# An extra 4 KB load of w1, issued by ACT between its two x loads, in a LayerNorm-MLP kernel

## The chip, the cores and the metric

The kernel runs on one core of a Trainium2 chip. A core has five engines with instruction queues of their own: TensorE (PE in the profile; its weight loads are listed apart as PEld), VectorE (DVE), ScalarE (ACT), GpSimd (POOL) and SyncE (SP). Transfers between DRAM and the on-chip memory (SBUF) are issued by an engine's queue and carried out by 16 DMA engines. Engines wait for one another through semaphores. The metric is the device time of one execution in microseconds, lower is better; the median of three runs is given.

## What is computed

x is 1 x 2048 x 1024, w1 is 1024 x 3584, w2 is 3584 x 1024, all in bf16.

```python
def reference(x, w1, b1, w2, b2):
    y = _layernorm(x, axis=-1)
    h = _gelu(jnp.einsum("bsd,df->bsf", y, w1) + b1)
    return jnp.einsum("bsf,fd->bsd", h, w2) + b2
```

The LayerNorm has no scale or shift of its own (eps 1e-5), and the GELU is the tanh form.

## The kernel before

The 2048 rows of x are 16 tiles of 128 rows; four tiles make a block of 512. The 1024 columns are eight row blocks of w1 ("t" or "dt", 128 rows each, 128 x 3584 x 2 = 917,504 bytes apart in DRAM), and the 3584 hidden columns are 28 groups "r" of 128. For each block of x the kernel makes the first product for all 28 groups (`pe_cell`, L330: w1 is the stationary operand, the transposed tile yT the moving one, eight matmuls to a group), applies bias and GELU on ACT (L350) into hT, and makes the second product (`out_chunk`, L379), to which DVE adds b2 (L390) before SP stores it. All of w1, w2 and x stay in SBUF once loaded.

The order on every engine is written by hand into five programs (`sp`, `pe`, `act`, `dve`, `pool`), lists of operations with the names of the events they wait for and signal. `_resolve` turns each name into a semaphore and a count, and `_emit` writes each list out in order: an engine stops at an operation until the events it names are there. `dma(dst, src, sig, nbytes, q)` (L177 and L178) appends one load to the SP list, or to the queue given as `q`, with a semaphore of its own. `est`, which `dma` fills from the sum of bytes, is a planned time by which the DVE's later operations are interleaved (L521 to L536); the first tiles' order does not depend on it.

**The loads at the start.** x tiles 0 and 1 come in halves of 512 columns: SP issues x0_0 and x1_0, ACT issues x0_1 and x1_1 (L200 to L203). Then, all on SP: w1 chunks 0, 1 and 2 (w1c0 to w1c2: two row blocks each, the first 512 columns; L204), x tile 2, w1c3, x tile 3, w1c4 and w1c5 (columns 512 to 768), b1, the other w1 chunks, x block 1, w2 in four chunks, b2, and x blocks 2 and 3.

**The first tile's way.** After its loads ACT loads its activation table (L399) and sums the first half of x tile 0 (L400); DVE sums the other half (L402) and subtracts the mean (L407, y0, in two parts). For tile 1 DVE makes the sum (L412) and the centred tile (L416, y1), in `raw_tile`; tile 2 follows in the same way. Tiles 0 to 2 of the first block are multiplied without their scale, which DVE applies to the product later (L347).

**The PE's opening.** 37 fill matmuls on constants (L290), the transposes of tile 0 (T0, L304), and then the steps of `OPEN` (L22): an entry (t, a, b) stands for tile t's matmuls with row blocks a to b for four groups r, and (t, None) for the transposes of tile t (T1, T2). ACT copies each transposed group from PSUM into yT (L310).

```python
OPEN = ((0, 0, 2), (1, None), (0, 2, 4), (0, 4, 6), (1, 0, 6), (0, 6, 8), (2, None), (1, 6, 8), (2, 0, 8))
```

So the (0,0,2) cells need w1c0, the (0,2,4) cells w1c1, the (0,4,6) cells w1c2 and the (0,6,8) cells w1c3; T1 needs y1, and T2 needs y2.

Of the kernel before, what the change touches and what calls it, by code (L numbers as in the profile page):

```python
# [7 lines left out]
BF16 = mybir.dt.bfloat16  # L8
# [3 lines left out]
P = 128  # L12
# [12 lines left out]
GROUPS_1 = ((0, 4, 6), (4, 8, 7))  # L25
GROUPS_2 = ((0, 2, 4), (2, 5, 5), (5, 8, 6))
NOB = 2
TAIL_CUTS = (0, 384, 512)
N_W2_CHUNKS = 4

# [56 lines left out]
def bass_standalone__mixer_channel_mlp__prompt_kernel(  # L87
# [13 lines left out]
    DT = D // P  # L101
# [32 lines left out]
    w1v = w1.rearrange("(t p) f -> p t f", p=P)  # L134
    w2v = w2.rearrange("(t p) d -> p t d", p=P)

    with ExitStack() as es:
        sb = lambda name, shape, dt: es.enter_context(nc.sbuf_tensor(name, shape, dt))
# [5 lines left out]
        hT_sb = sb("hT_sb", [P, FT, TB], BF16)  # L144
        o_sb = sb("o_sb", [P, NOB, D], BF16)
        b2_sb = sb("b2_sb", [P, D], BF16)
        c_sb = sb("c_sb", [P, NRAW, D], BF16)
        b1r_sb = sb("b1r_sb", [32, P], BF16)
        b1h_sb = sb("b1h_sb", [P, 32], BF16)
        b1_sb = sb("b1_sb", [P, 32], F32)  # L150
        junk_a = sb("junk_a", [P, HC], BF16)
        junk_d = sb("junk_d", [P, HC], BF16)
        ident = sb("ident", [P, P], BF16)
# [14 lines left out]
        act = _Prog("s_act")  # L168
# [8 lines left out]
        def dma(dst, src, sig, nbytes, q=None):  # L177
            (q or sp).op(lambda e, dst=dst, src=src: e.dma_start(dst, src), sig=sig, sem="d_" + sig, inc=16)  # L178
            dma_bytes[0] += nbytes
            est[sig] = DMA_T0 + dma_bytes[0] / DMA_BYTES_PER_US  # L180
# [18 lines left out]

        for i in range(2):  # L200
            for h, q in enumerate((sp, act)):
                dma(x_sb[:, i, h * HC:(h + 1) * HC], xf[i * P:(i + 1) * P, h * HC:(h + 1) * HC],
                    f"x{i}_{h}", P * HC * 2, q)  # L203
        for ci in range(3):  # L204
# [164 lines left out]
        def out_chunk(b, st, c0, c1, region, prev_store):  # L369
            ti = b * TPB + st  # L370
            ob = ti % NOB
            g = grp_n[0]
            grp_n[0] += 1
            bank = NRING + g % 2
            sig = f"m2_{ti}_{c0}"
            waits = [f"w2c{ci}" for ci in range(nw2c)]
            waits.append(grp_oe[g - 2] if g >= 2 else bank_gelu[bank])
            for ft in range(FT):
                pe.op(lambda e, st=st, ft=ft, c0=c0, c1=c1, bank=bank: e.matmul(  # L379
                    ps[:, bank, 0:c1 - c0], lhsT=hT_sb[:, ft, st * P:(st + 1) * P], rhs=w2_sb[:, ft, c0:c1],  # L380
                    start=(ft == 0), stop=(ft == FT - 1)),
                    waits=(waits if ft == 0 else []) + [hT_row[(b, ft)]],
                    sig=(sig if ft == FT - 1 else None))
            pe_t[0] += FT * _mm_us(c1 - c0)
            est[sig] = pe_t[0]
            dwaits = [sig, "b2"]
            if prev_store is not None:
                dwaits.append(prev_store)
            oe = f"oe_{ti}_{c0}"
            crit.append((est[sig], (lambda e, ob=ob, c0=c0, c1=c1, bank=bank: e.tensor_tensor(  # L390
                out=o_sb[:, ob, c0:c1], in0=ps[:, bank, 0:c1 - c0], in1=b2_sb[:, c0:c1], op=ALU.add),
                dwaits, oe, 0.2 + (c1 - c0) * 1e-3), b))
            grp_oe.append(oe)
            sev = f"st_{ti}_{c0}"
            sp.op(lambda e, ti=ti, ob=ob, c0=c0, c1=c1: e.dma_start(of[ti * P:(ti + 1) * P, c0:c1], o_sb[:, ob, c0:c1]),
                  waits=[oe], sig=sev, sem=f"d_st_{ob}_{region}", inc=16)
            store_last[(ob, region)] = sev
# [96 lines left out]
        for b in range(NB):  # L494
# [11 lines left out]
            for st in range(TPB):  # L506
                for dh in range(DH):
                    c0, c1 = dh * NCH, (dh + 1) * NCH
                    ob = (b * TPB + st) % NOB
                    prev = store_last.get((ob, dh))  # L510
                    last = (b == NB - 1 and st == TPB - 1 and dh == DH - 1)
                    if last:
                        for k, (a0, a1) in enumerate(zip(TAIL_CUTS[:-1], TAIL_CUTS[1:])):
                            out_chunk(b, st, c0 + a0, c0 + a1, dh if k == 0 else f"{dh}p{k}", prev)
# [65 lines left out]
```

## Time and profile before

| | before |
|---|---|
| median of 3 runs | 398.07 us (397.82 to 398.11) |
| profiled execution: its own time | 398.39 us |
| profiled execution: span | 397.2 us |
| granted TensorE clock | 1.00 |
| PE busy | 392.3 us (99%) |
| DVE, ACT, POOL busy | 156.6, 82.7, 9.5 us |
| DMA packets, bytes | 17357, 23.62 MB |
| HBM read, written | 19.14 MB, 4.19 MB |

The span is the time from the first to the last instruction that the profiler recorded; the execution's own time also holds what lies around it, here 1.19 us. The load engines are busy nearly all of the first 50 us, as the page's slices show, of 9.9 us each:

```profile
DMA  8999940000000000000000000000000000000000
GB/s 257 353 386 386 387 164 15 26 26 16 26 1 2 0 0 2 27 15 26 26 15 0 0 2 0 11 17 26 15 26 13 2 0 0 2 13 26 15 26 26
```

The row for the loads by queue shows who issues: q1 is SP's queue, q10 is ACT's, and q8 and q14 are fetches of instructions:

```profile
q1 hardware_dynamic: 17050, 23.08, 16.7%
q8 instruction: 15, 0.25, 0.3%
q10 hardware_dynamic: 288, 0.26, 0.2%
q14 instruction: 4, 0.03, 0.0%
```

ACT's 288 packets are the 256 pieces of x0_1 and x1_1, of 1 KB each, and 32 packets that report their arrival (16 to a load).

### The profile page before, as it was taken

Reading aid. Unit: us, or ns where it says so; the run is one execution under the profiler, and the core shown is the slowest. Engines: PE = TensorE matmul, PEld = TensorE weight load, DVE = VectorE, ACT = ScalarE, POOL = GpSimd, SP = SyncE. Lnnn points to the kernel's source line nnn. Section 1 sums busy time; section 2 is a strip of 40 time slices with the busy share of each in tenths; the row PEclk is TensorE's granted clock in tenths of the full one; section 3 lists DMA queues with packets and bytes.
Section 4 is the critical chain, followed back from the end, with each engine's and each line's share of the span. In section 5 each row is a group of like instructions: output and inputs, shape, how many; then the busy total and the mean of one; then the engine's idle time right before and its main releaser. Section 6 shows DMA issues by size and latency. Waiting matters only on the chain.

```text
span 397.2 us, 4608 instructions
## 1 busy us (share of the span) xinstructions
PE 392.3 (99%) x1968; PEld 187.9 (47%) x2003; DVE 156.6 (39%) x341; ACT 82.7 (21%) x125; POOL 9.5 (2%) x25
## 2 busy tenths in 40 slices
PE   8999999999999999999999999999999999999998
PEld 8844444444444444444444444444444444444445
DVE  4957889988999405988100000001100000001011
ACT  4264430000134442000024433100003334400000
POOL 0201100011000100000000000000000000000000
DMA  8999940000000000000000000000000000000000
GB/s 257 353 386 386 387 164 15 26 26 16 26 1 2 0 0 2 27 15 26 26 15 0 0 2 0 11 17 26 15 26 13 2 0 0 2 13 26 15 26 26
DMA packets 17357, 23.62 MB, mean 59 GB/s; under 512 B 1082, under 2 KB 9786, under 8 KB 17338
## 3 DMA queue, kind: packets, MB, share of 16 engines
q1 hardware_dynamic: 17050, 23.08, 16.7%
q8 instruction: 15, 0.25, 0.3%
q10 hardware_dynamic: 288, 0.26, 0.2%
q14 instruction: 4, 0.03, 0.0%
HBM read 19.14 MB, written 4.19 MB: 59 GB/s over the span
## 4 chain that ended last, share of the span: by engine, by line
PE 97%; DMA 1%; issue 1%; SPq 0%; DVE 0%
PE ps L379 49%; PE ps L330 48%; DMA w_sb<-in_w_dram 1%; SPq L178 0%; PE ps L304 0%; DVE o_sb L390 0%
## 5 line engine op out<-in xcount | busy, mean ns | idle before, releaser
L330 PE MATMUL ps<-yT_sb,w_sb 128*128 128x512 bf16 (+2 forms) x989 | 193.9, 355 | 1.2
L379 PE MATMUL ps<-w_sb,hT_sb 128*128 128x512 bf16 (+2 forms) x908 | 193.3, 373 | 0.8
L330 PEld LDWEIGHTS ps<-yT_sb,w_sb 128*128 128x128 bf16 x1008 | 92.5, 98 | 101.4 <-DMA w_sb<-in_w_dram 0.6
L379 PEld LDWEIGHTS ps<-w_sb,hT_sb 128*128 128x128 bf16 x924 | 89.2, 98 | 104.5
L350 ACT ACTIVATE hT_sb<-ps,b_sb 128x512 bf16<-128x512 f32 x112 | 76.2, 688 | 255.9 <-PE ps L330 231.8
L390 DVE TENSOR_TENSOR o_sb<-ps,b_sb 128x512 bf16<-128x512 f32 (+2 forms) x33 | 22.3, 675 | 198.9 <-PE ps L379 198.8
L277 DVE STREAM_TRANSPOSE yT_sb<-x_sb 32x256 bf16<-32x256 bf16 x192 | 83.7, 436 | 21.6 <-PE ps L330 18.6
L231 DVE BATCH_NORM_STATS2 st_sb<-x_sb 128x6 f32<-128x512 bf16 x32 | 20.9, 668 | 0.1
L347 DVE TENSOR_TENSOR ps<-ps,rbc_sb 128x384 f32<-128x384 f32 x28 | 15.2, 563 | 9.4 <-PE ps L330 9.0
L235 POOL TENSOR_TENSOR rstd_sb<-mv_sb,nhalf 128x1 f32<-128x1 f32 x16 | 8.7, 549 | 124.2 <-DVE mv_sb L238 124.1
L245 DVE TENSOR_SCALAR x_sb<-x_sb,mv_sb,rstd_sb 128x1024 bf16<-128x1024 bf16 x13 | 7.1, 545 | 2.8 <-POOL rstd_sb L235 2.0
L310 ACT COPY yT_sb<-ps 128x384 bf16<-128x384 bf16 (+2 forms) x10 | 4.5, 504 | 6.8 <-PE ps L304 6.8
L290 PE MATMUL ps<-const-bfloat16-1.0 128*128 128x128 bf16 x39 | 4.5, 310 | 0.8 <-PEq L565 0.8
L290 PEld LDWEIGHTS ps<-const-bfloat16-1.0 128*128 128x128 bf16 x39 | 4.1, 145 | 0.8 <-issue 0.8
L238 DVE BATCH_NORM_AGGREGATE mv_sb<-st_sb 128x2 f32<-128x15 f32 x16 | 3.5, 217 | 0.8
L304 PE MATMUL ps<-ident,c_sb 128*128 128x128 bf16 x24 | 2.4, 249 | 0.1
L402 DVE TENSOR_SCALAR_CACHE_REDUCE junk_d<-x_sb 128x512 bf16<-128x512 bf16 x1 | 0.7, 686 | 3.7 <-DMA x_sb<-in_x_dram 3.7
L304 PEld LDWEIGHTS ps<-ident,c_sb 128*128 128x128 bf16 x24 | 1.8, 111 | 0.3 <-issue 0.3
L412 DVE SCALAR_TENSOR_TENSOR junk_d<-x_sb 128x512 bf16<-128x512 bf16 x2 | 1.4, 688 | 1.1 <-DMA x_sb<-in_x_dram 1.1
L399 ACT ACT_TABLE_LOAD x1 | 1.3, 1283 | 1.7 <-PEq L565 1.7
L446 DVE STREAM_TRANSPOSE rbc_sb<-rs_sb 32x96 f32<-32x96 f32 x4 | 1.1, 270 | 0.1
L416 DVE TENSOR_SCALAR c_sb<-x_sb,sum_sb 128x1024 bf16<-128x1024 bf16 x2 | 1.0, 487 | 0.1
(22 smaller groups left out, 6.8 us busy)
## 6 DMA issues: line engine op xcount, KB each, us to landing
w_sb<-in_w_dram SPq DMA_DIRECT2D x4, 1792.0 KB, 18.5
w_sb<-in_w_dram SPq DMA_DIRECT2D x2, 2048.0 KB, 14.4
out_dram<-o_sb SPq DMA_DIRECT2D x31, 128.0 KB, 1.7
x_sb<-in_x_dram SPq DMA_DIRECT2D x3, 1024.0 KB, 14.5
w_sb<-in_w_dram SPq DMA_DIRECT2D x6, 256.0 KB, 5.5
w_sb<-in_w_dram SPq DMA_DIRECT2D x1, 1024.0 KB, 9.3
x_sb<-in_x_dram SPq DMA_DIRECT2D x2, 256.0 KB, 5.7
w_sb<-in_w_dram SPq DMA_DIRECT2D x1, 512.0 KB, 6.4
```

The lines of the kernel that those rows point to most:

```text
L231: return (lambda e, i=i, h=h: e.bn_stats(st_sb[:, i, 6 * h:6 * (h + 1)], x_sb[:, i, h * HC:(h + 1) * HC]), [x_ev.get(i, f"x{i}_{h}")], f"s ...
L235: pool.op(lambda e, i=i: e.tensor_tensor(out=rstd_sb[:, i:i + 1], in0=mv_sb[:, i, 1:2], in1=nhalf[:, i:i + 1], op=ALU.pow), waits=[f"mv{i} ...
L245: return (lambda e, i=i: e.tensor_scalar(out=x_sb[:, i, :], in0=x_sb[:, i, :], scalar1=mv_sb[:, i, 0:1], scalar2=rstd_sb[:, i:i + 1], op0= ...
L277: res.append((lambda e, src=src, dst=dst: e.transpose(out=dst, in_=src), waits, (f"tr{i}" if lastop else None), 0.47))
L290: pe.op(lambda e: e.matmul(ps[:, 0, 0:P], lhsT=one, rhs=one, start=True, stop=True), waits=[gate] if gate else [])
L304: pe.op(lambda e, j=j, o=(j - j0) * P: e.transpose(out=bap[:, o:o + P], in_=src[:, j * P:(j + 1) * P], identity=ident[:, :]), waits=waits, ...
L310: act.op(lambda e, dst=dst, psrc=psrc: e.copy(out=dst, in_=psrc), waits=[f"tp{i}_{j0}"], sig=f"te{i}_{j0}")
L330: pe.op(lambda e, b=b, r=r, dt=dt, n0=n0, n1=n1, bank=bank: e.matmul(ps[:, bank, n0:n1], lhsT=w1_sb[:, dt, r * P:(r + 1) * P], rhs=yT_sb[: ...
L347: crit.append((est[sig], (lambda e, bank=bank: e.tensor_tensor(out=ps[:, bank, 0:n], in0=ps[:, bank, 0:n], in1=rb, op=ALU.mult), [sig, "rb ...
L350: act.op(lambda e, r=r, bank=bank: e.activation(out=hT_sb[:, r, :], in_=ps[:, bank, :], func=ACT.Gelu_apprx_tanh, bias=b1_sb[:, r:r + 1], ...
L379: pe.op(lambda e, st=st, ft=ft, c0=c0, c1=c1, bank=bank: e.matmul(ps[:, bank, 0:c1 - c0], lhsT=hT_sb[:, ft, st * P:(st + 1) * P], rhs=w2_s ...
L390: crit.append((est[sig], (lambda e, ob=ob, c0=c0, c1=c1, bank=bank: e.tensor_tensor(out=o_sb[:, ob, c0:c1], in0=ps[:, bank, 0:c1 - c0], in ...
```

## The change

One load is added to ACT's list, between x0_1 and x1_1. It reads 16 elements (32 bytes) from each of 16 rows (every eighth) of each of the eight row blocks of w1, 128 pieces and 4096 bytes in all, into a new tile `touch_sb` of 16 partitions. Nothing reads this tile, and nothing waits for its semaphore. ACT issues x1_1 and all that follows after it.

```diff
+TOUCH = 16
...
+        touch_sb = sb("touch_sb", [16, DT, TOUCH], BF16)
...
         for i in range(2):
             for h, q in enumerate((sp, act)):
+                if i == 1 and q is act:
+                    dma(touch_sb[:, :, :], w1v[0:P:P // 16, :, 0:TOUCH], "touch", 16 * DT * TOUCH * 2, q)
                 dma(x_sb[:, i, h * HC:(h + 1) * HC], xf[i * P:(i + 1) * P, h * HC:(h + 1) * HC],
                     f"x{i}_{h}", P * HC * 2, q)
```

`w1v` is w1 seen as `(t p) f -> p t f` with p = 128 (L134), so partition p of the touch holds row 8p of every row block.

## The prediction

> **What bounds the kernel now.** I read the chain of waits first, then the start of that chain in order of time, then the start of all engines, then the load engines in short stretches. The page's chain:
>
> ```profile
> PE 97%; DMA 1%; issue 1%; SPq 0%; DVE 0%
> PE ps L379 49%; PE ps L330 48%; DMA w_sb<-in_w_dram 1%; SPq L178 0%; PE ps L304 0%; DVE o_sb L390 0%
> ```
>
> 97% is matmul. The change touches none of it, so only the other 3% can move. In order of time (start, length, what):
>
> ```profile
> 1.64 0.05 issue
> 1.69 0.43 SPq L178
> 2.12 0.04 issue
> 2.16 0.47 SPq L178
> 2.63 0.04 issue
> 2.67 5.29 DMA w_sb<-in_w_dram
> 7.96 0.05 issue
> 8.00 2.41 PE ps L330 x40
> ```
>
> The third w1 piece (w1c2, issued by SP at 2.67) lands at 7.96 and releases the PE at 8.00; from there the chain is PE to the end, but for gaps of 0.05 and the last store. So the end moves one for one with the PE's start at 8.00, and nothing after it can be won by this change. The timeline up to there (start, length, instruction, idle time before):
>
> ```profile
> 0.78 0.89 ACTq L178 DMA_DIRECT2D x_sb<-in_x_dram  x2
> ...
> 1.70 1.28 ACT L399 ACT_TABLE_LOAD   x1 [1.70 <-PEq L565]
> ...
> 3.57 0.63 ACT L400 ACTIVATE junk_a<-x_sb 128x512 bf16<-128x512 bf16 x1 [0.58 <-DMA x_sb<-in_x_dram]
> ...
> 5.20 0.68 DVE L412 SCALAR_TENSOR_TENSOR junk_d<-x_sb 128x512 bf16<-128x512 bf16 x1
> ...
> 6.41 0.64 PE L330 MATMUL ps<-yT_sb,w_sb 128*128 128x128 bf16 x8
> 6.83 0.49 PEld L304 LDWEIGHTS ps<-ident,c_sb 128*128 128x128 bf16 x8
> ```
>
> Issues and landings by the DMA view: ACT issues x0_1 at 0.78 (0.41 us) and x1_1 at 1.22 (0.46); x1_1 lands 3.4 us later, at 4.62. w1c0, w1c1, w1c2 land at 6.39, 7.26 and 7.96 (issue at 1.69, 2.16, 2.67 plus 4.7, 5.1, 5.3). The load engines in stretches of half a microsecond (the last two columns are their busy share and GB/s):
>
> ```profile
> 1.75:2.25 0.50, 0.50 (x7) 0.50 (x6) 0.00 (x0) 0.50 (x1) 0.00 (x0) 1.00 0.82 45
> ...
> 2.75:3.25 0.50, 0.50 (x8) 0.50 (x6) 0.00 (x0) 0.23 (x1) 0.00 (x0) 1.00 1.09 377
> 3.25:3.75 0.50, 0.50 (x7) 0.50 (x6) 0.01 (x1) 0.18 (x1) 0.00 (x0) 1.00 1.04 295
> 3.75:4.25 0.50, 0.50 (x8) 0.50 (x6) 0.50 (x1) 0.50 (x2) 0.00 (x0) 1.00 0.92 248
> 4.25:4.75 0.50, 0.50 (x7) 0.41 (x4) 0.39 (x3) 0.04 (x1) 0.00 (x0) 1.00 0.95 285
> ```
>
> Two cold starts show here. In 1.75 to 2.25 the engines are 82% busy and move 45 GB/s: the DMA view of that stretch has 22 packets at 81.8% of 16 engines, so 0.818 x 16 x 0.5 / 22 = 0.30 us for each 1 KB piece, the first of x. And from 3.25, when w1's first pieces come up, the rate falls to 295, 248, 285, then 324 and 326, and is 358 on average from 5.75 to 8.25; the shortfall is (63+110+73+34+32) x 0.5 / 358 = 0.44 us. It isn't even: by the sums of these rates the bytes of x0, x1 and w1c0 (786 KB) have moved by about 4.85, but w1c0 lands at 6.39, 1.5 us later, while x1 landed 0.7 us after its bytes. The trace's arrival times agree: 14 of w1c0's 16 parts arrive by 5.37, two at 6.35 and 6.36. This lag of about a microsecond on two engines stays with w1c1 and w1c2, and so sets the 8.00.
>
> **The change part by part.** Removed: nothing. Added: one issue on ACT, 128 pieces of 32 bytes and 16 arrivals on the load engines; moved: x1_1's issue and what ACT does after it.
>
> ACT's issue: the nearest rows are the other L178 issues, 0.41 to 0.57 us while the queue is open, and 1.20 for b1 (28 pieces, at 5.87, with a backlog ahead). I take 0.45. Queued behind it on ACT: x1_1's issue (1.22 to 1.67), the table load (1.70 to 2.15, end 3.43) and L400, which waits for x0_0 until 3.57. The 0.58 idle hides it: cost 0. At 1.20 the table load would end at 4.18 and y0 come 0.55 late; the PE has 0.4 us between its T0 transposes (the last starts near 6.0) and 6.41, and 0.2 before 8.00, so even that ends near 0.
>
> x1_1: lands at 4.62 + 0.45 = 5.07 if the touch itself takes little. L412 for tile 1 begins at 5.20, when the DVE is free, so it is hidden. After that cover, L412 (0.69 + 0.08) and L416 (0.49) give y1 at 6.41, and T1 is loaded at 6.83: another 0.42. So x1_1 may land as late as about 5.6 before T1 is late, and T1 may be 0.2 late before w1c2's matmuls are.
>
> The touch on the load engines: 8 pieces and one arrival on each. Lower bound: 256-byte pieces in the last store, 144 packets at 18.7% of 16 engines over 0.8 us, 0.187 x 16 x 0.8 / 144 = 17 ns each; nine on each engine are 0.15 us. Upper bound: x's first pieces, 0.30 us; eight are 2.4 us. Engines are busy from 1.75 on (0.98 of 1.70 to 8.20), so this is paid by the SP queue's loads too, w1c2 among them. In the stretch 2.25 to 3.25 SP's queue has 55.8% and ACT's 37.9% of the same 16 engines.
>
> A rule that speaks against the change: the Trainium skill, "DMA: Bandwidth & Descriptors", section "Issuing engines are not separate DMA queues", says that loads issued from any engine run on the same 16 engines and interleave, so another issuer saves issue time only. By it the touch delays SP's loads by its own time; with engines of its own the sum would be 0 for them; the two shares just named agree with the rule.
>
> The planned times: `dma` adds the 4096 bytes to its sum, so every later load's `est` moves by 4096 / 0.34e6 = 0.012 us. At most a transpose of x and a scaling change places in the DVE's list; DVE is busy 39% of the span and the chain has it with the last add alone: 0.
>
> What it spares: w1c0 and w1c1 read row blocks that the touch has already read from; at most the 0.44 us shortfall and the lag of two engines. But the touch can't begin before ACT's x0_1 pieces are through, near 3.0, and w1c0 begins near 3.4: there is no idle time in which a slow first read is free. An engine that is held by the touch's first read is held for x1_0 and w1c0 too (at 1.75 to 2.25 only SP's queue has packets, though ACT issued at the same time). So I take the first reads as moved by 0.4 us, not saved: 0, bounds -0.65 (below) and 0.
>
> Sum: ACT 0, x1_1 0, pieces +0.15, first reads 0: w1c2 at 8.11, PE at 8.15. Against the profiled execution, 397.2 span plus 1.19 around it = 398.39, that is 398.54; the median of the runs is 0.32 lower, so 398.07 + 0.15 = **398.2**. Its own range is 397.9 to 398.9: the two lagging engines may gain or lose some tenths.
>
> **The rivals.** *The first reads are spared* (faster). The touch asks for all eight row blocks in a short time, and if the slow reads overlap, w1c0 to w1c2 arrive as on the 14 good engines. For it: the two late parts, and that the later w1 columns, read from the same blocks, run at 387 GB/s. Against: w2 and x's later blocks are also first reads and run at 387 with no dip. Price: with w1c0 to w1c2 in time, the PE does its (0,0,2) cells from 6.05, T1 from 6.50 (y1 is there at 6.41), the (0,2,4) cells from 6.95 and the next at 7.35, not 8.00: at most -0.65. Less the pieces and a rest of the lag, -0.45: 397.6.
>
> *Each of the touch's reads is a slow one* (slower). Its place is the ACT queue ahead of x1_1, on all 16 engines. Eight row blocks 917 KB apart are eight first reads; if each holds its engine for the 0.30 us of x's first pieces, that is 2.4 us, less the 0.44 spared: w1c2 lands at 9.9, PE +1.9, 400.0. y1 would come at 4.62 + 0.45 + 2.4 + 1.26 = 8.7, T1 thus 1.9 late as well. It decides from the fifth of the eight reads: 4 x 0.30 - 0.44 = +0.75, about the 0.8 us that is 0.2%. For it: x's first reads did just this on all engines. Against: x's cost only one or two pieces on each engine, and w1's whole first use costs 0.44, not 2.4; but w1c0 reads pieces one after the other in one block, where the touch changes block each time.
>
> The Trainium skill, "HBM Reference", section "Latency", gives an access 0.2 us on average and 2 us at high load. By the second figure one held read alone is, as an estimate, +1.6 and 399.6; the 0.30 of x's pieces lies by the first, and no row here shows a read of 2 us.
>
> *It does nothing*: nobody waits for the touch, its pieces are 4 KB of 23.62 MB, and they fall into the shares that the engines leave (0.92 and 0.95 in 3.75 to 4.75): 398.07.
>
> **How the numbers follow.** Chances: moved reads 0.36 (398.2), spared 0.26 (397.6), slow reads 0.32 (400.0, less with fewer held), nothing 0.06 (398.07). About 0.2% (0.8 us) is what a measurement of this kernel can tell from no change. Slower by more: all of slow reads and 0.05 of the moved ones' upper end, 0.37. Faster by more: the -0.65 is from one execution, others may lose more at their start, so 0.10 of the spared ones. Within: 0.53. The range runs from 397.3 (the spared case's bound and a little) to 400.1 (eight slow reads).
>
> **What would show it.** Right: ACT's third issue of 0.4 to 0.6 us, L400 still at 3.57, L412 for tile 1 at 5.2 to 5.6, w1c2's landing at 8.0 to 8.2, and every PE line after it shifted alike. Spared: the rate from 3.25 to 5.75 stays near 358, w1c0 lands near 5.5 and the PE's 40 matmuls begin at 7.4 to 7.7. Slow: a stretch with busy engines and few GB/s near 3, x1_1 after 6, the 40 matmuls after 8.8. My forecast is wrong if the PE's start there moves by over 0.8 us either way, or if the end moves and that start doesn't.

## The result, and the profile after

The change costs three quarters of a microsecond: 398.81 us (median of 21 runs, 398.39 to 399.11) against 398.05 (21 runs, 397.77 to 398.57), a ratio of 1.0019 with a 95% interval of 1.0012 to 1.0025. Its profiled execution took 398.72 us (span 397.5), that of before 398.39 (span 397.2).

The page's chain of the changed kernel, by engine and by line; its lines stand two further down at L178 and four further from L204 on, so L334 and L383 are the two products, L308 the transposes, L416 and L420 tile 1's sum and centred tile:

```profile
PE 98%; DMA 1%; DVE 0%; ACTq 0%; issue 0%; DVEq 0%
PE ps L383 49%; PE ps L334 49%; DMA x_sb<-in_x_dram 1%; PE ps L308 0%; ACTq L180 0%; DVE junk_d L416 0%; DVE c_sb L420 0%; DVE o_sb L394 0%; DVEq L75 0%
```

The 1% of loads is no longer of w1 but of x. The same chain in order of time (start, length, what):

```profile
0.78 0.40 ACTq L180
1.18 0.03 issue
1.21 0.47 ACTq L180
1.67 0.03 issue
1.70 4.34 DMA x_sb<-in_x_dram
...
6.14 0.71 DVE junk_d L416 x2
6.85 0.02 issue
6.88 0.50 DVE c_sb L420
7.37 0.05 issue
7.42 0.62 PE ps L308 x8
8.04 2.68 PE ps L334 x48
10.72 0.45 PE ps L308 x8
```

It runs through ACT's three issues to x1_1, issued at 1.70 and landed at 6.04, then through y1 (done at 7.37) to T1 at 7.42. Before, x1_1 landed at 4.57 by the trace's arrivals (the prediction's 4.62 added a rounded 3.4 to the issue), y1 was done at 6.41 and T1 was loaded at 6.83. The timeline of the same stretch (start, length, instruction, idle time before it and what ended it):

```profile
2.18 1.28 ACT L403 ACT_TABLE_LOAD   x1 [2.18 <-issue]
...
3.48 0.63 ACT L404 ACTIVATE junk_a<-x_sb 128x512 bf16<-128x512 bf16 x1
...
6.14 0.69 DVE L416 SCALAR_TENSOR_TENSOR junk_d<-x_sb 128x512 bf16<-128x512 bf16 x1 [1.07 <-DMA x_sb<-in_x_dram]
...
7.42 0.62 PE L308 MATMUL ps<-ident,c_sb 128*128 128x128 bf16 x8 [0.41 <-DVE c_sb L420]
```

DVE now idles 1.07 us for x1_1, and the PE idles for y1. The touch's issue is about as short as the others, 0.47; ACT's sum of x0 starts no later than before. The load engines (last two columns: busy share and GB/s):

```profile
3.25:3.75 0.50, 0.50 (x7) 0.50 (x6) 0.21 (x1) 0.49 (x2) 0.00 (x0) 1.00 0.55 52
3.75:4.25 0.50, 0.50 (x8) 0.50 (x6) 0.48 (x2) 0.45 (x2) 0.00 (x0) 1.00 0.57 150
```

The rate where w1 starts, 295 and 248 GB/s in 3.25 to 4.25 before, is now 52 and 150, and x1_1 stands in the middle of it. Two readings offer themselves: the touch's own reads slow the engines, or x1_1, issued 0.48 later, has merely slipped from its place ahead of w1c0's slow start into it.

### The profile page after: what moved, and what is told of

It is laid out like the page before. It is cut to its first block, busy times and chain, and to the rows that moved or that the text cites. A ratio compares the mean times of both kernels' runs of the same rounds, so it can differ in the third digit from the quotient of the medians.

```text
span 397.5 us, 4644 instructions
## 1 busy us (share of the span) xinstructions
PE 394.2 (99%) x2003; PEld 188.2 (47%) x2003; DVE 156.6 (39%) x341; ACT 82.7 (21%) x125; POOL 9.5 (2%) x25
## 4 chain that ended last, share of the span: by engine, by line
PE 98%; DMA 1%; DVE 0%; ACTq 0%; issue 0%; DVEq 0%
PE ps L383 49%; PE ps L334 49%; DMA x_sb<-in_x_dram 1%; PE ps L308 0%; ACTq L180 0%; DVE junk_d L416 0%; DVE c_sb L420 0%; DVE o_sb L394 0%; DVEq L75 0%
## 5 line engine op out<-in xcount | busy, mean ns | idle before, releaser
L334 PE MATMUL ps<-yT_sb,w_sb 128*128 128x512 bf16 (+2 forms) x1008 | 195.0, 356 | 0.2 <-DMA w_sb<-in_w_dram 0.2
L383 PE MATMUL ps<-w_sb,hT_sb 128*128 128x512 bf16 (+2 forms) x924 | 194.1, 373 | 0.0
L334 PEld LDWEIGHTS ps<-yT_sb,w_sb 128*128 128x128 bf16 x1008 | 92.7, 98 | 101.2 <-DMA w_sb<-in_w_dram 0.4
L383 PEld LDWEIGHTS ps<-w_sb,hT_sb 128*128 128x128 bf16 x924 | 89.3, 98 | 104.4
L308 PE MATMUL ps<-ident,c_sb 128*128 128x128 bf16 x24 | 2.4, 248 | 0.4 <-DVE c_sb L420 0.4
L308 PEld LDWEIGHTS ps<-ident,c_sb 128*128 128x128 bf16 x24 | 1.7, 110 | 0.7 <-DVE c_sb L420 0.6
L416 DVE SCALAR_TENSOR_TENSOR junk_d<-x_sb 128x512 bf16<-128x512 bf16 x2 | 1.4, 682 | 1.1 <-DMA x_sb<-in_x_dram 1.1
L420 DVE TENSOR_SCALAR c_sb<-x_sb,sum_sb 128x1024 bf16<-128x1024 bf16 x2 | 1.0, 486 | 0.1
```

The lines of the kernel that those rows point to most:

```text
L308: pe.op(lambda e, j=j, o=(j - j0) * P: e.transpose(out=bap[:, o:o + P], in_=src[:, j * P:(j + 1) * P], identity=ident[:, :]), waits=waits, ...
L334: pe.op(lambda e, b=b, r=r, dt=dt, n0=n0, n1=n1, bank=bank: e.matmul(ps[:, bank, n0:n1], lhsT=w1_sb[:, dt, r * P:(r + 1) * P], rhs=yT_sb[: ...
```

## The experiments

Times are medians. Ratios are to runs of the kernel before on the same chip, with a 95% interval; they are worked out from the single runs and are not quotients of two medians. The medians of the kernel before were 398.30 us beside the first four experiments, 398.21 beside sixteen pieces, the delay, the touch with x1_1 by SP and w1 held back, and 398.08 beside the others. Theory 1 is that the change loses its time by x1_1's late landing; rival 2, that the tiny pieces cost the load engines the same wherever they stand; rival 3, that reading w1's row blocks is what costs.

### The touch behind x1_1

```diff
-                if i == 1 and q is act:
-                    dma(touch_sb[:, :, :], w1v[0:P:P // 16, :, 0:TOUCH], "touch", 16 * DT * TOUCH * 2, q)
                 dma(x_sb[:, i, h * HC:(h + 1) * HC], ...
+                if i == 1 and q is act:
+                    dma(touch_sb[:, :, :], w1v[0:P:P // 16, :, 0:TOUCH], "touch", 16 * DT * TOUCH * 2, q)
...
+        sp.op(None, waits=["touch"])
```

> The touch is issued by ACT after x1_1 instead of before it (and SP waits for its arrival at the very end, where it has long been there). Theory 1 (the change lost its time because x1_1 landed late, 6.04 instead of 4.62, and y1 and T1 with it): x1_1 lands by 4.9, tile 1's sum starts on DVE by 5.3, T1 by 6.9, and the time is 397.6 to 398.2. Rival 2 (the touch's tiny pieces cost the load engines the same wherever they stand) and rival 3 (the PE's opening still hangs on the w1 loads, which the touch delays): 398.5 to 398.9 as with the change, with w1c2 landing at 8.2 or later.

398.06 us, ratio 1.0002 (0.9984 to 1.002). By the trace's arrivals x1_1 lands at 4.45, and in the chain T1 begins at 6.48:

```profile
6.48 0.62 PE ps L308 x8
```

The interval is too wide to tell this time from the change's 1.0019; the landing and T1's start do tell. The same load behind x1_1 makes neither late: its place decides, not the pieces or the blocks. Nothing is seen to be won either.

### The touch of x tile 0's rows

```diff
-                    dma(touch_sb[:, :, :], w1v[0:P:P // 16, :, 0:TOUCH], "touch", 16 * DT * TOUCH * 2, q)
+                    dma(touch_sb[:, :, :], xf[0:P:P // 16, :].rearrange("p (t c) -> p t c", t=DT)[:, :, 0:TOUCH], "touch", 16 * DT * TOUCH * 2, q)
```

> Same place, same 128 pieces of 32 bytes, but read out of the rows of x tile 0, which the load just ahead of it on ACT's queue has begun to read. Theory 1, with the slow part being first reads of w1's row blocks: the late issue stays (about 0.48), the slow reads go; x1_1 lands at 5.0 to 5.4, T1 starts by 6.9, time 397.9 to 398.3. Rival 2 (the pieces' own cost): x1_1 lands near 6, time 398.6 to 398.9.

398.81 us, ratio 1.0006 (0.999 to 1.0022; the runs of before on this chip hold four at 400.2 to 400.5 and scatter widely). x1_1 lands at 6.32 and T1 starts at 7.71, with this piece in the chain:

```profile
1.70 4.62 DMA x_sb<-in_x_dram
```

The time alone is not clear of noise, the landing is. The expectation that I held was wrong: without any early read of w1, x1_1 is as late as with the change. That takes the slow reads of the touch out of the theory (rival 3 falls), and left two: the pieces (rival 2), or, **theory 1b**, x1_1's later issue alone, which puts it beside w1c0's first reads.

### The touch within one row block

```diff
-                    dma(touch_sb[:, :, :], w1v[0:P:P // 16, :, 0:TOUCH], "touch", 16 * DT * TOUCH * 2, q)
+                    dma(touch_sb[:, :, :], w1[0:P, 0:TOUCH].rearrange("(p e) f -> p e f", e=DT), "touch", 16 * DT * TOUCH * 2, q)
```

> Same place, 128 pieces of 32 bytes out of the 128 rows of w1's row block 0 alone, eight neighbouring rows to each engine. If each row block costs a slow first read (theory 1 in its sharpest form), there is one slow read to an engine and not up to eight: x1_1 at 5.2 to 5.7, time 398.0 to 398.5, and w1c1 lands with its tail as before (7.2). Rival 2: 398.6 to 398.9.

400.43 us, ratio 1.0046 (1.0027 to 1.0065): the time was missed by every theory, and the landing of x1_1 by the sharpest form of theory 1. x1_1 lands at 6.38, not at 5.2 to 5.7, and T1 begins at 7.76, much as in the run before it. (The touch's own issue took 0.65 us here, so that x1_1 was issued at 1.91.) What differs most is the PE's granted clock (the last column but two):

```profile
7.25:7.75 0.50, 0.00 (x0) 0.00 (x0) 0.50 (x2) 0.00 (x0) 0.00 (x0) 1.00 1.07 397
7.75:8.25 0.50, 0.49 (x6) 0.49 (x7) 0.50 (x2) 0.00 (x0) 0.00 (x0) 0.67 1.06 383
8.25:8.75 0.50, 0.50 (x8) 0.50 (x6) 0.50 (x2) 0.45 (x1) 0.00 (x0) 0.50 1.07 392
11.00:11.50 0.50, 0.50 (x9) 0.50 (x7) 0.50 (x2) 0.00 (x0) 0.00 (x0) 0.67 1.20 290
```

By the means of these stretches the clock falls to half at about 7.9 and comes back at about 11.3: the transposes of T1 take 0.93 in the chain, not 0.62, and the 48 matmuls behind them 4.00, not 2.68, together 1.6 us. Six of this kernel's twelve runs have a mean clock of 0.996 and lie at 400.7 to 401.7; the other six, at 1.0, lie at 398.9 to 400.2. So the time of the profiled run speaks of the clock and not of row blocks. The clock is not all of it: the six runs at 1.0 have a median of 399.6, 0.8 above the change, and the profile, taken at 0.996, doesn't show why.

### The kernel before, again

The kernel before, without an edit.

> The kernel before once more, for a second profile of its start and for the scatter of the comparison. Ratio 1.000 within 0.001. If the profiled start that was shown (two engines late by a microsecond, w1c2 at 7.96) was an unlucky one, w1c2 lands earlier here and the PE's first matmuls of tile 1 begin before 8.4.

397.85 us, ratio 0.999 (0.9971 to 1.0009). Its profiled execution took 397.81 (span 396.5), and its chain in order of time holds no load at all:

```profile
0.82 4.11 PE ps L290 x37
4.93 0.10 issue
5.03 0.37 PE ps L304 x2
5.40 0.21 PE ps L290 x2
5.61 0.57 PE ps L304 x6
6.19 0.45 PE ps L330 x8
6.63 0.45 PE ps L304 x8
7.08 2.72 PE ps L330 x48
9.80 0.45 PE ps L304 x8
```

The PE goes from its fill matmuls to the end without waiting for a load. By the trace's arrivals w1c2 lands at 7.35 here (7.96 in the first profile), and tile 1's transposes are done by 7.1. The execution on which I made the sum was one in which w1's first reads went badly. The slow start is there in this one too, a microsecond later (238 and 178 GB/s in 4.25 to 5.25), but the PE is not held by it.

### Sixteen pieces

```diff
-                    dma(touch_sb[:, :, :], w1v[0:P:P // 16, :, 0:TOUCH], "touch", 16 * DT * TOUCH * 2, q)
+                    dma(touch_sb[:, 0, :], xf[0:P:P // 16, 0:TOUCH], "touch", 16 * TOUCH * 2, q)
```

> Same place on ACT's queue, but 16 pieces of 32 bytes (one to an engine, out of x tile 0's rows) in place of 128. Theory 1b (after the touch of x0 cost as much as the touch of w1): not the pieces cost, but that x1_1 is issued half a microsecond later and so meets w1c0's slow first reads on the same engines; x1_1 lands at 5.6 to 6.4 and the time is 398.4 to 399.0 as with the change. Rival 2 (the tiny pieces hold the engines): an eighth of the pieces, x1_1 at 5.0 to 5.3, time 397.9 to 398.3.

398.68 us, ratio 1.0011 (0.9999 to 1.0022), and in the chain:

```profile
1.69 4.33 DMA x_sb<-in_x_dram
...
7.40 0.62 PE ps L308 x8
```

4.33 with 16 pieces of x, 4.34 with 128 pieces of w1: the pieces cost nothing that shows, and rival 2 falls.

### A delay without a load

```diff
+                if i == 1 and q is act:
+                    for k in range(2):
+                        act.op(lambda e, k=k: e.copy(out=dly_sb[:, k, :], in_=one), sig=f"dly{k}")
+                    act.op(None, waits=["dly1"])
```

(`dly_sb` is a new tile, and `one` the constant.)

> No touch at all: ACT makes two small copies of a constant and waits for them between the issues of x0_1 and x1_1, so that x1_1 is issued some 0.4 to 0.7 later. Theory 1b: the lateness alone does it; x1_1 lands at 5.5 to 6.4, T1 at 7.2 to 7.8, time 398.4 to 399.0. Rivals 2 and 3 (pieces, or the touch's first reads of w1): x1_1 at 5.0 to 5.3, T1 as before, time 397.8 to 398.3.

403.24 us, ratio 1.0126 (1.0106 to 1.0146), but the dose was not the one I meant: the copies brought a table load of 1.28 us with them, x1_1 was issued at 3.03 and landed at 7.82, a second table load made the sum of x0 late as well, and four of five runs have a reduced mean clock. A late issue hurts, and the size says nothing on the change.

### x1_1 by SP, ahead of w1c0, with the touch and without

```diff
-                    f"x{i}_{h}", P * HC * 2, q)
+                    f"x{i}_{h}", P * HC * 2, sp if i == 1 else q)
```

The first run makes this edit to the change (and adds a wait of SP for the touch at the very end), the second to the kernel before.

> The touch stays where it is on ACT, and SP issues x1_1 right behind x1_0, ahead of w1c0 (so the w1 loads are issued 0.45 later; SP waits for the touch's arrival at the very end). Theory 1b: x1_1 is ahead of w1 again and lands by 5.0, T1 by 6.9, time 397.7 to 398.4. Rival 2 or 3 (the touch holds the engines): x1_1 after 5.6, time 398.5 or more.

> No touch; SP issues x1_1 behind x1_0 and ahead of w1c0, so at the same 1.7 as the change's ACT does. Theory 1b: being issued at 1.7 does not hurt when w1c0 stands behind it; x1_1 lands by 5.2, T1 is not late for y1, and the time is that of f3_x1_on_sp less the touch, 398.0 to 398.5. If a late issue costs by itself: x1_1 at 5.6 or later and 398.5 or more.

With the touch 398.46 us, ratio 1.0004 (0.9995 to 1.0013); without 398.52, ratio 1.001 (1.0001 to 1.0019). By the trace's arrivals x1_1, issued at 1.69 as in the change, lands at 5.21 and 5.40, not at 6.04, and tile 1's sum on DVE starts accordingly (with the touch L416, without it L412):

```profile
5.31 0.69 DVE L416 SCALAR_TENSOR_TENSOR junk_d<-x_sb 128x512 bf16<-128x512 bf16 x1
...
5.50 0.69 DVE L412 SCALAR_TENSOR_TENSOR junk_d<-x_sb 128x512 bf16<-128x512 bf16 x1 [0.26 <-DMA x_sb<-in_x_dram]
```

A late issue costs far less when w1c0 stands behind it. Both landings, and the 398.46, are a little over what I expected; without the touch one of 16 parts came 0.8 after the others, and DVE waited 0.26 us. What remains of the time lies with the w1 loads, each issued half a microsecond later: the chain of the run with the touch goes by w1c0 (issued at 2.16), that of the run without it by w1c3 (issued at 4.17, landed at 9.71). The two runs differ by less than their intervals, so no cost of the touch shows between them.

### w1 held back until x1_1 has landed

```diff
+        sp.op(None, waits=["x1_1"])
         for ci in range(3):
             load_w1(ci)
```

> The change, and SP holds w1c0 and all behind it until x1_1 has landed. The w1 loads come some 3 us later, so the time is worse under every theory (400 to 402); what is read is x1_1's landing. Theory 1b: with the touch ahead of it but no w1 load beside it, x1_1 lands at 4.8 to 5.3. Rival 3 (the touch's own first reads of w1's row blocks hold the engines): 5.7 or later, with a stretch of few GB/s before it.

400.81 us, ratio 1.0077 (1.0052 to 1.0101), and in the chain, with the touch ahead of x1_1 as in the change:

```profile
1.70 3.03 DMA x_sb<-in_x_dram
...
5.68 4.76 DMA w_sb<-in_w_dram
```

3.03 and not 4.34: without w1c0 beside it x1_1 lands at 4.72, behind the touch as it is, and takes no longer than at its old place (3.35 and 3.17 in the two profiles of the kernel before). By the trace's packets x1_1's 128 pieces begin between 3.53 and 4.34 here, with no piece of SP's loads among them; in the change they begin between 3.17 and 5.52, with 357 of SP's among them, and before between 3.24 and 4.16, with 117. The run shows one thing more. The touch has landed at 4.09, w1c0 is issued at 4.74, and yet w1 starts slowly:

```profile
1.75:2.25 0.50, 0.50 (x7) 0.50 (x6) 0.00 (x0) 0.07 (x1) 0.00 (x0) 1.00 0.79 109
2.25:2.75 0.50, 0.50 (x8) 0.50 (x6) 0.00 (x0) 0.50 (x1) 0.00 (x0) 1.00 0.72 254
...
5.75:6.25 0.50, 0.40 (x4) 0.13 (x2) 0.46 (x4) 0.38 (x2) 0.00 (x0) 1.00 0.60 88
6.25:6.75 0.50, 0.00 (x0) 0.00 (x0) 0.50 (x2) 0.48 (x2) 0.00 (x0) 1.00 0.79 276
...
7.75:8.25 0.50, 0.50 (x11) 0.50 (x12) 0.00 (x0) 0.00 (x0) 0.00 (x0) 1.00 0.63 197
8.25:8.75 0.50, 0.50 (x13) 0.50 (x11) 0.00 (x0) 0.21 (x1) 0.00 (x0) 1.00 0.99 182
```

The engines move nothing from 4.75 to 5.75, until w1 comes up; then they move 88 and 276 GB/s in its first microsecond and 197 and 182 when its later blocks begin (7.75 to 8.75), and w1c2 takes 4.76 us from issue to landing. A touch of every eighth row of each block, landed 0.65 us before the issue, doesn't spare w1's slow start. How slow it would have been without the touch isn't shown, since no run holds w1 back without it; and x's own first microsecond (109 and 254 GB/s in 1.75 to 2.75) looks like w1's, so only the dip from 7.75 on, with the engines at work before it, sets w1 apart from any load after a pause.

### x1_1 behind w1c0, and x1_1 in two halves

Both without a touch; the first lets SP issue x1_1 behind w1c0, the second splits x1_1 so that its second half is ACT's third issue.

```diff
+                if i == 1 and q is act:
+                    load_w1(0)
...
-                    f"x{i}_{h}", P * HC * 2, q)
-        for ci in range(3):
+                    f"x{i}_{h}", P * HC * 2, sp if i == 1 else q)
+        for ci in range(1, 3):
```

> No touch; SP issues x1_1 behind w1c0 (near 2.2). Theory 1b: with no extra load at all, x1_1 falls behind w1's slow first reads, lands at 5.9 to 6.8, T1 at 7.3 to 8.2, time 398.5 to 399.5. Rivals 2 and 3 (it takes the touch's pieces): x1_1 at 5.2 to 5.6, time 397.9 to 398.4.

```diff
-                dma(x_sb[:, i, h * HC:(h + 1) * HC], xf[i * P:(i + 1) * P, h * HC:(h + 1) * HC],
-                    f"x{i}_{h}", P * HC * 2, q)
+                c0 = h * HC
+                if i == 1 and q is act:
+                    dma(x_sb[:, i, c0:c0 + HC // 2], xf[i * P:(i + 1) * P, c0:c0 + HC // 2], "x1_1a", P * HC, q)
+                    c0 += HC // 2
+                dma(x_sb[:, i, c0:(h + 1) * HC], xf[i * P:(i + 1) * P, c0:(h + 1) * HC],
+                    f"x{i}_{h}", P * ((h + 1) * HC - c0) * 2, q)
...
-        raw_tile(1, ["x1_0", "x1_1"])
+        raw_tile(1, ["x1_0", "x1_1a", "x1_1"])
```

> No touch; ACT issues x1_1 as two loads of 256 columns, so that its second half is issued where the change issues x1_1 (1.7), with no byte more. Theory 1b: the second half lands at 5.5 to 6.3, T1 at 7.0 to 7.7, time 398.3 to 399.0. Rivals 2 and 3: as before, 397.8 to 398.2.

398.88 us, ratio 1.002 (1.0012 to 1.0029), and 398.64, ratio 1.0016 (1.0007 to 1.0024). The chain of the first, and behind it the load in that of the second:

```profile
2.15 3.87 DMA x_sb<-in_x_dram
...
7.40 0.62 PE ps L306 x8
```

```profile
1.70 4.49 DMA x_sb<-in_x_dram
```

x1_1 lands at 6.02 and T1 starts at 7.40, and in the second at 6.19 and 7.60: the change's loss, without a byte of the touch.

### The change, again

The changed kernel, without a further edit.

> The change once more, on the same chip as the three above, with a second profile of its start. Theory 1b: x1_1 lands near 6 again, T1 is released by y1 at 7.2 to 7.8, time 398.5 to 399.0, and it scatters less than the kernel before, since the PE waits for x1_1 whether w1's first reads go well or badly.

398.80 us, ratio 1.0021 (1.0011 to 1.0031), x1_1 issued at 1.70 and landed at 6.05, T1 at 7.43. The start of w1 differs from the first profile (177 and 219 GB/s in 3.25 to 4.25, not 52 and 150), the landing of x1_1 does not. The scatter was 398.44 to 400.56, against 397.62 to 398.91 of before, but the 400.56 alone was a run at a mean clock of 0.996; the eleven at 1.0 end at 399.36. So the expectation on the scatter is neither shown nor refuted.

## Why the prediction was right in its range, and where it was not

**The bound.** That the end follows the PE's start on tile 1 held. T1's 48 matmuls follow 8.04 in the chain of the change and 7.08 in the second profile of before, 0.96 later, and the executions differ by 398.72 - 397.81 = 0.91. Against the first profile it holds too: T2's transposes, which end this stretch, start at 10.72 in the change and at 8.00 + 2.41 = 10.41 there, 0.31 apart, and the executions differ by 0.33. That w1c2 sets this start was true of the first profiled execution alone; in the other none of the loads does. Of the 0.65 us that the prediction put down as the most that could be won there, that execution had 398.39 - 397.81 = 0.58 without any change.

**ACT's issue**, taken as 0.45 and free: measured 0.47 and free. The cover was used up, as x tile 0 came earlier (L400's counterpart started at 3.48, not at 3.57) and the table load ended at 3.46.

**x1_1: the term that was mis-sized.** "Lands at 4.62 + 0.45 = 5.07 if the touch itself takes little" carried the 3.4 us from issue to landing over from its old place, and the sum put the term at 0. It landed at 6.04, 4.34 after its issue, though the touch takes little: its 128 pieces took 7 to 9 ns each in the trace, 0.07 us on each engine. What I left out is which other load is in line at 1.70. At 1.22 x1_1 was ahead of w1c0 (1.69), at 1.70 beside it, and the w1 start that I had read in the same rows (0.44 us over all engines, a microsecond on the worst) then falls on x1_1. The limit that I gave, about 5.6 before T1 is late, was a little too wide, since DVE started 0.10 after the landing and T1 0.05 after y1; the landing passed it by 0.44, and T1 came at 7.42 instead of 6.83. The touch of x's rows, sixteen pieces, x1_1 behind w1c0, and x1_1 in two halves each reproduce it, the last two without a touch; w1 out of the way undoes it.

**The pieces**, taken as 0.15: nothing that shows. The rule of the Trainium skill that stood beside them, in "DMA: Bandwidth & Descriptors", section "Issuing engines are not separate DMA queues", bears on the term above instead: a load of ACT's is held up by SP's w1, with which it shares the engines, 4.34 us against 3.03 with w1 held back.

**First reads moved, not saved**, 0: right in its size, not in its reason. With w1 held back until the touch had landed, w1 started slowly all the same, and the touch behind x1_1 changed nothing that shows: no row shows a slow read that was moved.

**The rivals.** *Spared* (397.6) is refuted by the time, and the run with w1 held back shows the slow start behind the touch. With x1_1 issued by SP, w1c0 took 4.30 us from issue to landing with the touch and 4.04 without: nothing spared shows there either. The touch behind x1_1 can't tell, as its interval reaches down to 0.9984, which is 0.6 us. *Slow reads* (400.0) had the place right, ahead of x1_1 on ACT's queue, and the mechanism wrong: reads of x's own rows do the same. *It does nothing* is true of the touch's bytes and false of its issue. The sum came out as +0.15 and the measurement as +0.76, inside the case's own range; the sign was right by a term that I had set to nothing, and that is luck. The signs say so too: of those for *right*, ACT's third issue (0.45) came true, while L412's counterpart began at 6.14 instead of 5.2 to 5.6 and w1c2 landed at 7.65 instead of 8.0 to 8.2. Two of the signs of *slow reads* came true instead, x1_1 after 6 and a stretch of few GB/s, though with the engines only 55% busy.

## What to carry to other kernels

Here a load's time from issue to landing went by its place in line and not by the load alone: when something pushes it back, look for what is issued in the interval that it loses, on every queue, and price it beside that. A half-microsecond issue of four kilobytes cost more than its bytes here, because the load behind it was the one the next stage waited for, and it slipped level with the start of a heavy stream. And take the bound from two profiles when the chain hangs on a load: this one stood on a landing that varied by 0.6 us between executions.

## What had not been expected of the hardware

w1's first pieces are slow whether or not the same rows' neighbours have just been read: 88 and 276 GB/s in the first microsecond of w1, and 197 and 182 in 7.75 to 8.75, a microsecond after that, with the touch long landed and nothing else on the engines but x tile 2; 387 is reached later on. By the trace's packets it is a few pieces that are slow: of the 178 that began in 5.5 to 6.75, nine took over 0.15 us, up to 0.49, and the median was 0.046. From 8.30 on single 2 KB pieces of x tile 2, which shared the engines with w1c2, took up to 0.68 too, where 0.08 is usual, so the slowness is not w1's alone. What makes them slow wasn't found; x's blocks and w2, also read for the first time, showed no such dip.

The PE's granted clock can fall to half without a long idle time. In the touch of one block the PE waited 0.66 and 0.59 us, with work between, and had 0.50 of the clock from about 7.9 to 11.3, which cost 1.6 us; in the touch of x's rows it waited as long (0.83 and 0.45) and kept 1.00, and with w1 held back it waited 1.51 and 1.32 and kept 1.00. Four of 35 runs of the kernel before had a mean clock of 0.996 as well, with 400.2 to 400.5 us; they left no profile. What decides it was left open.
